# Rescheduling a Gram product and a triangular solve among the matmuls of a fused delta-rule attention and two-layer MoE kernel

## The chip, the cores and the metric

The kernel runs on one core of one Trainium2 chip. The metric is the time of one execution on the device in microseconds; the figure before is the median of three executions.

## The reference

A delta-rule attention (4 batches, 8 heads, 768 tokens, head dimension 48) feeds two dense layers that act on each token:

```python
for t in range(S):
    kt, vt, bt = (k_n[:, :, t], v[:, :, t], beta[:, :, t, None])
    y[:, :, t] = np.einsum('bhd,bhde->bhe', q[:, :, t], state)
    v_old = np.einsum('bhde,bhd->bhe', state, kt)
    state = state + bt[:, :, :, None] * np.einsum('bhd,bhe->bhde', kt, vt - v_old)
...
h = np.maximum(x @ w_in, 0.0)              # 384 -> 2048
x = (h * h @ w_out)                        # 2048 -> 384
...
h = np.maximum(np.maximum(x @ w1, x @ w2), x @ w3)   # 384 -> 768
out = h @ w_out                            # 768 -> 384
```

## The kernel before

The 768 tokens are cut into 12 chunks of 64 (numbered 0 to 11). Inside a chunk the recurrence becomes a triangular system: the Gram matrix K K^T of the chunk, scaled by beta and by the key norms, is inverted, and the inverse is used in a handful of small matmuls. All dense matmuls run as three products of high and low parts, which is why tiles come in pairs (`xh`, `xl`; `gh`, `gl`).

The main loop runs over the chunks c. In round c, `moe_a(c)` runs the first dense layer on chunk c, while the attention of chunk c+1 and the preparation of later chunks are threaded between its steps. `moe_a` has eight blocks of the hidden dimension. `s1(f)` (L599) is 18 matmuls into one of two banks `p1`; ACT takes them through relu, square and a rounding to `gh` (L605 to L607) and DVE forms `gl` (L608), after which the bank is free. `s2(f)` (L619) multiplies `gh` and `gl` into the accumulator `px`, two blocks later. At the end DVE transposes `px` to `xs` (L639), which frees `px` and is stored.

`moe_a` yields after every `s1` and `s2`; the yields are numbered: step 1 follows s1(0), 2 s1(1), 3 s1(2), 4 s2(0), 5 s1(3), 6 s2(1), 7 s1(4), 8 s2(2), 9 s1(5), 10 s2(3), 11 s1(6), 12 s2(4), 13 s1(7), 14 s2(5), 15 s2(6), and step 16 follows s2(7) and the transposes to `xs`. `steps` takes lists of step numbers, each with a generator, and advances the generator once for each occurrence of the step. `pin` then orders the instructions of PE and DVE exactly as they were written; ACT, POOL and the DMA queue of SP are ordered by the scheduler.

The generators that matter here:

- `attention(c+1)`: loads of the inverse (`load_x`, POOL's queue, L348 and L366), products with the state (st0), `zz` (a DVE transpose `xT`, L419, and the matmuls `pZ`, L426, copied to `z` by ACT, L427), `ww` (the matmuls `pW`, L436, which read `xT` and `z`), `mm_u` (L491), st2 (L543, L521; DVE then adds to `Sb`, L528, and copies `yy`, L553), st3 (PE transposes `yy` to `pT`, L561; the results are `xh` and `xl`, L564 and L565). In even rounds these stand at steps 1, 2, 4, 6, 8, 11, 13; in odd rounds at 1, 2, 5, 7, 10, 12, 14 (round 9: 6 and 8 in place of 5 and 7).
- `kkps`: four Gram products (two chunks, two halves), each in two pieces. The first piece is 64 small matmuls into two banks `pk` and `pq` (L182), an ACT copy (L198) and a DVE multiplication with the mask (L199); the second is the stores on SP's queue (L186, L206). The banks come from the pool `ps_at` of two, which the attention uses as well.
- `solve32(g)`: the inverse of the 32x32 diagonal blocks of two chunks. Its first piece loads the Gram blocks to `M32` (L312, SP's queue). The second is the preparation `prep`: the diagonal `ss` (L247), a square root on ACT (L218), a selection on POOL (L236), some short DVE operations and two of 1024 elements (L247 to L255). Then come 30 pairs of DVE operations (L292, L293), a memset and a last scaling (L295, L296), with a PE transpose of the norms (`pt`, L279) among them; then the result goes to DRAM (`xt`, L329), from where the next round's `load_x` fetches it.

Rounds 3, 5 and 7 run `kkps` and the first piece of `solve32`; rounds 4, 6 and 8 run the rest of that solve; rounds 5, 7 and 9 fetch its result. Round 2 has a list of its own. After chunk 11 the second layer (L1023, L1040) runs on the tokens alone.

Of the kernel before, what the change touches and what calls it, by code (L numbers as in the profile page):

```python
# [35 lines left out]
HALVED = [(c, c + 1) for c in range(0, NC, 2)]  # L36
# [3 lines left out]
def delta_moe(ctx, tc, kc, ab, kt, vt, beta, beta32, beta16, kq, w_in, w_out, w1, w2, w3, w_out2, out):  # L40
# [124 lines left out]
    def kkp_load(c, p, dma=nc.sync):  # L165
        k = kcts[nk[0] % len(kcts)]
        nk[0] += 1
        kcs[c, p] = k
        i = dma.dma_start(k, two(kc, c, p).rearrange("p b q t s -> p (b q) t s"))
        for j in kc_after:  # L170
            behind(i.ins, j)

    def kk_matmul(c, p, ps_, swap=1):

        k = kcs.pop((c, p))
        pk, pq = (ps_[0].tile([128, U2, C], F32, name=n, tag=ps_[1]) for n in ("pk", "pq"))
        for u in range(U2):
            for i, ps in enumerate((pk, pq)):
                for t in range(2):
                    r = slice(64 * t, 64 * t + D)  # L180
                    o = 64 * (t ^ i * swap)
                    pe.matmul(ps[o:o + 64, u], k[r, u, 0], k[r, u, i], start=True, stop=True)  # L182
        return pk, pq

    def kk_store(c, p, kk, dma=nc.sync):
        dma.dma_start(kk_d[c // 2].rearrange("t j c u i -> (t j) c u i")[:, c % 2, U2 * p:U2 * p + U2], kk)  # L186

    def kkps(cs, ps_, dma=nc.sync):

        todo = [(c, p) for c in cs for p in range(2)]  # L190
        ahead = len(kcts) - (len(kcts) < 4)
        for n in range(min(ahead, len(todo))):
            kkp_load(*todo[n], dma)
        for n, (c, p) in enumerate(todo):
            ks = kss[nk[1] % len(kss)]
            nk[1] += 1
            pk, pq = kk_matmul(c, p, ps_[n % len(ps_)])
            kk_ends[0] = act.copy(ks[:, 0], pk).ins  # L198
            kk_ends[1] = vec.tensor_mul(out=ks[:, 1], in0=pq, in1=mask.unsqueeze(1).broadcast_to([128, U2, C])).ins  # L199
            for i in mul_after:  # L200
                behind(kk_ends[1], i)
            yield
            kk_store(c, p, ks[:, 0], dma)

            for t in range(2):
                dma.dma_start(p_d[c][64 * t:64 * t + 64, U2 * p:U2 * p + U2], ks[64 - 64 * t:128 - 64 * t, 1])  # L206
            if n + ahead < len(todo):
                kkp_load(*todo[n + ahead], dma)
            yield
# [63 lines left out]
    def behind(ins, before):  # L273

        tc.add_manual_dep(ins, before.name, mybir.DependencyInfo(mybir.DependencyClass.NoSync, mybir.DependencyReason.DATA), reason="order")
# [378 lines left out]
    def steps(main, *others):  # L654

        due = [0.0] * len(others)
        for n, _ in enumerate(chain((None,), main)):
            pin()
            for i, (rate, g, *_) in enumerate(others):
                due[i] += rate.count(n) if isinstance(rate, list) else rate * (n > 0)  # L660
                while due[i] >= 1.0:
                    due[i] -= 1.0
                    next(g, None)
                    pin()
        for rate, g, *keep in others:
            for _ in () if keep else g:
                pin()
# [7 lines left out]
    def w3load(ws):  # L675
        todo = []

        def turned():
            if after:
                after[:], abs_after[:] = last_gl, last_gh  # L680
            raw, i, fs = todo.pop(0)
            turn(raw, wh[i][:, :, fs], wl[i][:, :, fs], vec)

        for i in ws:
            w = (late if i < 2 else wb).tile([128, 2, KD, F2], F32R, name=f"w3_{i}", tag="ABC"[i])
            wh[i], wl[i] = w[:, 0], w[:, 1]
            for f in range(NF2):
                fs = slice(128 * f, 128 * (f + 1))
                todo.append((fetch(w3s[i][:, :, 256 * f:256 * (f + 1)], (KD, 128), nc.sync), i, fs))
                if len(todo) > 1:  # L690
                    turned()
                yield
        turned()
# [29 lines left out]
    def part(g, n):  # L723
        for _ in range(n):
            next(g, None)
            yield
# [5 lines left out]
    if True:  # L732
# [20 lines left out]
        def solve32(g, load=(nc.sync, nc.sync), landing=0):  # L753
            M, a, ready, norm = start32(g, load) if g else begun
            for _ in range(landing):
                yield
            if landing:
                prep_after[:] = last_gl
            nm = ready()
            if not g:  # L760
                normed.append(lambda: norms_at.append(norm(nm)))
            yield
            for n, i in enumerate(solve(vec, M, 32, 64 * len(HALVED[g]), a, tmp32, g < 2)):
                for j in solve_after:
                    behind(i.ins, j)
                ops.append(i.ins)
                if g and n == (24 if g == 1 else 8):
                    norm(nm)
                yield
            i = finish32(g, M)  # L770
            if i:
                ops.append(i)

        def later(n, g):
            for _ in range(n):
                yield
            yield from g
# [3 lines left out]
        def weights(first, each):  # L781
            n = first
            while queue:
                if last_gl[0] and last_gl[0] not in gls:
                    gls.append(last_gl[0])
                after[:] = gls[-2:-1] or last_vec[:1]
                words(n)
                n = each
                after.clear()
                prep_after[:] = solve_after[:] = parted[-1:]  # L790
                yield

        at, p1 = (ps_at, "at"), (ps_s1, "p1")
# [168 lines left out]
        KK = {1: 2, 3: 3, 5: 4, 7: 5}  # L962
        ahead_ = {}
        for c in range(NC):
            extra = []
            if c == 0:
                solve_next = solve32(1, (pool, pool))
                extra += [(11 / 15.0, later(3, attention(1))), (list(range(17)), weights(2, 2)), (4.0, later(20, part(solve_next, 10)))]
            elif c == 1:
                pinned.update({first_matmul.ins.engine: None, last_gl[0].engine: None})  # L970
                first_solve = [0] * 3 + [1 + n * 18 // 20 for n in range(20)]
                extra += [(first_solve, solve_next), ([13, 19, 22, 25, 27, 28, 30], attention(2))]
                ahead_[2] = solve32(2, landing=1)
                extra += [([9, 10, 16, 17, 20, 21, 24, 25], kkps(HALVED[2], (at,))), ([28], ahead_[2], True)]
                solve_after[:] = last_vec
                kc_after[:] = raws[-1:]
                prep_after.clear()
            elif c + 1 < NC:
                extra.append(([1, 2, 5 + c // 9, 7 + c // 9, 10, 12, 14] if c % 2 else [1, 2, 4, 6, 8, 11, 13], attention(c + 1)))
            if c == 2:  # L980
                kc_after.clear()
                solve_after.clear()
            if c in ahead_:
                extra.append(([2] + [3 + n * 12 // 32 for n in range(32)] if c == 2 else [3 + n * 12 // 33 for n in range(33)], ahead_[c]))
            if c > 1 and c in KK:
                extra.append(([4, 5, 6, 7, 9, 10, 11, 12], kkps(HALVED[KK[c]], (at,))))
                ahead_[c + 1] = solve32(KK[c], landing=1)
                extra.append(([12], ahead_[c + 1], True))
            if c == 9:
                after[:] = last_gl  # L990
                load_w3s = w3load((0, 1))
            if 9 <= c < NC - 1:
                extra.append((0.4, part(load_w3s, 6)) if c > 9 else (0.8, later(6, part(load_w3s, 6))))
            if c == NC - 1:
                pr.close()
                wb = ctx.enter_context(tc.tile_pool(name="wb", bufs=1, side="right", reuse_waits="tile"))
                first = []
                extra.append((0.6, chain(load_w3s, w3load((2,)))))
                extra.append((0.5, later(2, x2_steps(0, wb, first))))
            steps(moe_a(c, gp, c == 1), *extra)  # L1000
# [114 lines left out]
```

## Time and profile before

| | |
|---|---|
| three executions | 911.59, 913.41, 913.48 us; median 913.41 |
| the profiled execution | 915.94 us, its span 913.8 |
| PE busy / DVE busy | 871.0 / 478.5 us |
| ACT busy / POOL busy | 387.8 / 135.7 us |

The span is the time between the first and the last instruction that the profile shows; a few microseconds lie around it. Rounds 3 to 9 take about 47 us each: round 3 starts near 208 us in the span, round 4 near 259, round 5 near 303, round 9 near 488. "Busy" counts compute instructions alone. A row that ends in `[1.32 <-DVE ...]` says that the engine idled 1.32 us before it and what it waited for.

### The profile page before, as it was taken

The page shows a single profiled execution, that of the slowest core. Times are in us where ns is not written, and L with a number is a line of the kernel's source. Part 1 is how long each engine was busy: PE and PEld are TensorE (multiplying, and loading weights), DVE is VectorE, ACT ScalarE, POOL GpSimd, SP SyncE. Part 2 cuts the span into 40 slices and gives each one's busy share as a digit, 9 for nine tenths or more (in the row PEclk, how much of TensorE's full clock was granted, in tenths as well). Part 3 has the DMA queues.
Part 4 walks back from the last instruction along what each step waited for, and adds up shares of the span by engine and source line. Part 5 has one row for each costly group of instructions (what it writes and reads, how often), then busy time and mean ns, then how long its engine had stood idle before and what let it go on. Part 6 is the DMA issues. An engine that isn't in the chain of part 4 may idle for free.

```text
span 913.8 us, 26365 instructions
## 1 busy us (share of the span) xinstructions
PE 871.0 (95%) x11414; PEld 845.0 (92%) x11414; DVE 478.5 (52%) x1069; ACT 387.8 (42%) x825; POOL 135.7 (15%) x226
## 2 busy tenths in 40 slices
PE   4589899999999999999999999999999999999998
PEld 4588899999998999999999899999999999999997
DVE  5887985694349524962496354566232332323221
ACT  6568745453445343534453566554121221222211
POOL 5041201223312231223122400001000000000000
PEclk8759999999999999999999999999999999999999
DMA  9968446525652566245715441434010101000000
GB/s 264 360 169 255 116 100 168 125 65 144 179 117 66 136 174 129 64 112 158 147 58 123 116 124 37 122 105 137 29 36 27 35 27 35 10 27 9 18 18 35
DMA packets 114035, 95.36 MB, mean 104 GB/s; under 512 B 69880, under 2 KB 95240, under 8 KB 113920
## 3 DMA queue, kind: packets, MB, share of 16 engines
q1 hardware_dynamic: 95232, 55.41, 23.0%
q0 software_dynamic: 11584, 32.64, 13.3%
q10 hardware_dynamic: 7104, 5.64, 2.0%
q8 instruction: 89, 1.46, 0.7%
q14 instruction: 26, 0.21, 0.1%
HBM read 70.45 MB, written 22.77 MB: 102 GB/s over the span
## 4 chain that ended last, share of the span: by engine, by line
PE 74%; DVE 14%; DMA 4%; ACT 3%; issue 3%; POOL 1%; ACTq 0%; DVEq 0%; POOLq 0%
PE p L1023 25%; PE p L599 16%; PE px L619 16%; PE po L1040 8%; DVE buf L292 3%; DVE buf L293 3%; DVE gl L608 2%; PE pk L182 2%; PE pU L491 1%; PE pY L543 1%; PE pA L467 1%; DMA raw<-in_moe_w_out_dram 1%; DMA p<-ksr 1%; PE pW L436 1%; DMA xb<-xt 1%
## 5 line engine op out<-in xcount | busy, mean ns | idle before, releaser
L1023 PE MATMUL p<-x_h,w 128*128 128x384 f32 x864 | 220.2, 336 | 0.0
L619 PE MATMUL px<-wout,gh 128*128 128x384 f32 x768 | 200.4, 342 | 1.5 <-ACT gh L607 0.8
L599 PE MATMUL p<-xh,win_h 128*128 128x256 f32 x576 | 169.3, 294 | 3.1 <-DVE gl L608 2.6
L599 PE MATMUL p<-xl,win_h 128*128 128x256 f32 x576 | 163.9, 284 | 0.2 <-DVE xl L565 0.2
L599 PE MATMUL p<-xh,win_l 128*128 128x256 f32 x576 | 163.8, 284 | 0.0
L1023 PEld LDWEIGHTS p<-x_h,w 128*128 128x128 f32 x864 | 156.2, 188 | 0.0
L1023 PE MATMUL p<-x_l,w 128*128 128x384 f32 x432 | 145.2, 336 | 0.0
L608 DVE TENSOR_TENSOR gl<-p,gh 128x512 fp32r<-128x512 f32 x96 | 66.2, 689 | 145.1 <-ACT gh L607 141.4
L619 PEld LDWEIGHTS px<-wout,gh 128*128 128x128 f32 x768 | 135.4, 190 | 3.4 <-issue 1.2
L619 PE MATMUL px<-wout,gl 128*128 128x384 f32 x384 | 129.4, 337 | 0.0
L605 ACT ACTIVATE p<-p 128x512 f32<-128x512 f32 x96 | 55.9, 582 | 172.1 <-PE p L599 169.4
L599 PEld LDWEIGHTS p<-xh,win_h 128*128 128x128 f32 x576 | 110.8, 192 | 6.7 <-DVE gl L608 3.3
L599 PEld LDWEIGHTS p<-xl,win_h 128*128 128x128 f32 x576 | 111.0, 193 | 0.5 <-DVE xl L565 0.4
L599 PEld LDWEIGHTS p<-xh,win_l 128*128 128x128 f32 x576 | 111.0, 193 | 0.0
L1029 DVE TENSOR_TENSOR mx<-p,mx 128x384 f32<-128x384 f32 x48 | 26.7, 557 | 128.1 <-PE p L1023 128.0
L1023 PEld LDWEIGHTS p<-x_l,w 128*128 128x128 f32 x432 | 81.2, 188 | 0.0
L1031 ACT CAST hh<-mx 128x384 fp32r<-128x384 f32 x48 | 24.6, 513 | 125.6 <-DVE mx L1030 125.6
L619 PEld LDWEIGHTS px<-wout,gl 128*128 128x128 f32 x384 | 72.7, 189 | 0.1
L293 DVE TENSOR_TENSOR buf<-buf 128x30 f32<-128x30 f32 (+9 forms) x180 | 59.7, 332 | 6.1
L292 DVE TENSOR_TENSOR buf<-buf 128x30 f32<-128x30 f32 (+9 forms) x180 | 59.4, 330 | 5.1
L607 ACT CAST gh<-p 128x512 fp32r<-128x512 f32 x96 | 56.4, 587 | 2.6
L606 ACT ACTIVATE p<-p 128x512 f32<-128x512 f32 x96 | 56.0, 583 | 2.7
(169 smaller groups left out, 1305.7 us busy)
## 6 DMA issues: line engine op xcount, KB each, us to landing
kq<-in_kc_dram POOLq DMA_DIRECT2D x20, 448.0 KB, 5.2
raw<-in_moe_w_dram SPq DMA_DIRECT2D x18, 384.0 KB, 3.7
raw<-in_moe_w_out_dram SPq DMA_DIRECT2D x16, 384.0 KB, 4.2
p<-p POOLq DMA_DIRECT2D x22, 256.0 KB, 4.0
rawp<-in_moe_w_in_dram SPq DMA_DIRECT2D x12, 384.0 KB, 7.0
v<-in_vt_dram POOLq DMA_DIRECT2D x24, 192.0 KB, 2.9
ktp<-in_kt_dram POOLq DMA_DIRECT2D x24, 192.0 KB, 4.0
x<-xs SPq DMA_DIRECT2D x48, 96.0 KB, 3.0
```

The source lines that it names most:

```text
L292: eng.tensor_tensor(out=tv, in0=col.unsqueeze(2).broadcast_to([u, k, l]), in1=row.unsqueeze(1).broadcast_to([u, k, l]), op=ALU.mult)
L293: i = eng.tensor_tensor(out=of_, in0=of_, in1=tv, op=ALU.add)
L599: pe.matmul(p1[:, j], w[:, k, f], x[c][:, k], start=n == 0 and j == 0, stop=n == 8, skip_group_check=True)
L605: act.activation(out=p1, in_=p1, func=AF.Relu)
L606: act.activation(out=p1, in_=p1, func=AF.Square)
L607: last_gh[0] = act.copy(gh, p1).ins
L608: last_gl[0] = vec.tensor_sub(out=gl, in0=p1, in1=gh.bitcast(F32)).ins
L619: g = pe.matmul(px[:, h, 0:DM], x[:, j, hs], w, start=f == 0 and i == 0, stop=f == NF - 1 and i == 2, skip_group_check=True)
L1023: pe.matmul(p, w[i][:, k, fs], x[:, k], start=n == 0, stop=n == 8)
L1029: vec.tensor_max(out=t, in0=ps[1], in1=t)
L1031: act.copy(hh[:, f], t2)
L1040: pe.matmul(po[:, 0:DM], x[:, f, js], w[:, f], start=i == 0, stop=i == 17)
```

## The change

Rounds 3, 5 and 7 (`c > 1 and c in KK`) and rounds 4, 6 and 8 (`c in ahead_`, other than 2) get new lists of steps:

```diff
-                extra.append(([2] + [3 + n * 12 // 32 for n in range(32)] if c == 2 else [3 + n * 12 // 33 for n in range(33)], ahead_[c]))
+                extra.append(([2] + [3 + n * 12 // 32 for n in range(32)] if c == 2 else [1 + n * 14 // 32 for n in range(32)], ahead_[c]))
             if c > 1 and c in KK:
-                extra.append(([4, 5, 6, 7, 9, 10, 11, 12], kkps(HALVED[KK[c]], (at,))))
+                extra.append(([4, 5, 6, 7, 8, 9, 9, 10], kkps(HALVED[KK[c]], (at,))))
                 ahead_[c + 1] = solve32(KK[c], landing=1)
-                extra.append(([12], ahead_[c + 1], True))
+                extra.append(([11, 15], ahead_[c + 1], True))
```

The matmuls of the third and fourth Gram product go from steps 9 and 11 to 8 and 9; their stores from 10 and 12 to 9 and 10; the load of `M32` from 12 to 11. The preparation, which was the first item of the next round (step 3), stands at step 15 of rounds 3, 5 and 7. The solve's operations in the next round are spread over steps 1 to 14 in place of 3 to 14. No instruction is added or removed.

DVE from the end of round 3, before (`xl` is the last operation of the attention, `xs` the transposes of `px`, `v` the products of st0):

```order
L565 TENSOR_TENSOR xl<-pT,xh 128x3x128 x2
L639 STREAM_TRANSPOSE xs<-px 128x384 x2
L608 TENSOR_TENSOR gl<-p_3991,gh 128x512
L608 TENSOR_TENSOR gl<-p_4030,gh 128x512
L458 TENSOR_TENSOR v<-v,normT 128x384
L471 TENSOR_TENSOR v<-v,pA 128x384
L458 TENSOR_TENSOR v<-v,normT 128x384
L471 TENSOR_TENSOR v<-v,pA 128x384
L608 TENSOR_TENSOR gl<-p_4131,gh 128x512
L247 COPY ss<-buf 128x32
```

and with the change:

```order
L565 TENSOR_TENSOR xl<-pT,xh 128x3x128 x2
L247 COPY ss<-buf 128x32
L219 SCALAR_TENSOR_TENSOR s_3977<-s_3977 128x32
L220 RECIPROCAL r<-s_3977 128x32
L221 TENSOR_TENSOR r<-r,ss 128x32
L222 SCALAR_TENSOR_TENSOR nm<-r,s_3977 128x32
L228 TENSOR_TENSOR s_3977<-nm 128x32
L229 RECIPROCAL a_3803<-s_3977 128x32
L230 SCALAR_TENSOR_TENSOR r<-b_3804,a_3803 128x32
L237 TENSOR_TENSOR buf<-buf,r 128x1024
L255 TENSOR_SCALAR a_3803<-r 128x32
L639 STREAM_TRANSPOSE xs<-px 128x384 x2
```

The preparation has moved from behind the third `gl` of round 4 to a place ahead of round 3's `xs`.

DVE around `xT` of round 4, before:

```order
L237 TENSOR_TENSOR buf<-buf,r 128x1024
L255 TENSOR_SCALAR a_3907<-r 128x32
L292 TENSOR_TENSOR buf<-buf 128x30
L293 TENSOR_TENSOR buf<-buf 128x30
L292 TENSOR_TENSOR buf<-buf 128x58
L293 TENSOR_TENSOR buf<-buf 128x2x29
L419 STREAM_TRANSPOSE xT<-x_4025 128x256
```

and with the change:

```order
L608 TENSOR_TENSOR gl<-p_4157,gh 128x512
L292 TENSOR_TENSOR buf<-buf 128x150
L293 TENSOR_TENSOR buf<-buf 128x6x25
L292 TENSOR_TENSOR buf<-buf 128x168
L293 TENSOR_TENSOR buf<-buf 128x7x24
L419 STREAM_TRANSPOSE xT<-x_4041 128x256
```

Between the third `gl` and `xT` there stood the whole preparation and two pairs of the solve; now two later pairs stand there.

ACT around the Gram copies of round 3 (`buf<-pk` and `big<-pk`, the third and fourth product), before:

```order
L445 COPY xb<-pW 32x8x32 x4
L607 CAST gh<-p_3540 128x512
L605 ACTIVATE p_3618<-p_3618 128x512
L606 ACTIVATE p_3618<-p_3618 128x512
L607 CAST gh<-p_3618 128x512
L198 COPY buf<-pk 128x512
```

and with the change:

```order
L445 COPY xb<-pW 32x8x32 x4
L607 CAST gh<-p_3540 128x512
L198 COPY buf<-pk 128x512
L605 ACTIVATE p_3654<-p_3654 128x512
L606 ACTIVATE p_3654<-p_3654 128x512
L607 CAST gh<-p_3654 128x512
L198 COPY big<-pk 128x512
```

The third copy has moved ahead of the copies of s1(5), and the fourth stands right behind them, ahead of the copies of `pU`.

## Rows read from the trace of the kernel before

**Rows 1.** The page, busy time of each engine (share of the span), instructions.

```profile
PE 871.0 (95%) x11414; PEld 845.0 (92%) x11414; DVE 478.5 (52%) x1069; ACT 387.8 (42%) x825; POOL 135.7 (15%) x226
```

**Rows 2.** Waits of PE, whole span: us in total, times, longest.

```profile
PE pW L436 <- DVE buf L292: 3.9, 3, 1.3
...
PE pT L561 <- DVE yy L553: 1.7, 3, 0.7
PE pZ L426 <- DMA xb<-xt: 1.3, 2, 0.8
```

**Rows 3.** Timeline of DVE in round 4: start, us, operation.

```profile
270.12 0.18 DVE L247 COPY ss<-buf 128x32 f32<-128x32 f32 x1
...
274.59 0.18 DVE L255 TENSOR_SCALAR a<-r 128x32 f32<-128x32 f32 x1
...
275.55 0.44 DVE L419 STREAM_TRANSPOSE xT<-x 128x256 f32<-128x256 f32 x1
```

**Rows 4.** Timeline of PE: a stall of round 3, two waits of round 4.

```profile
224.61 0.25 PE L426 MATMUL pZ<-xb,k 32*32 32x32 f32 x3 [1.20 <-issue]
...
276.13 0.74 PE L436 MATMUL pW<-k,xT 32*32 32x32 f32 x64 [1.32 <-DVE buf L292]
...
296.70 0.49 PE L561 MATMUL pT<-ident,yy 128*128 128x128 f32 x3 [0.72 <-DVE yy L553]
```

**Rows 5.** Groups of DVE, 274 to 306 us: busy, mean ns | idle before.

```profile
L293 DVE TENSOR_TENSOR buf<-buf 128x30 f32<-128x30 f32 (+14 forms) x30 | 10.0, 332 | 1.0
...
L608 DVE TENSOR_TENSOR gl<-p,gh 128x512 fp32r<-128x512 f32 x5 | 3.4, 683 | 0.0
```

**Rows 6.** Timeline of DVE from round 3 into round 4.

```profile
255.01 1.02 DVE L565 TENSOR_TENSOR xl<-pT,xh 128x384 fp32r<-128x384 f32 x2 [0.39 <-ACT xh L564]
258.99 1.05 DVE L639 STREAM_TRANSPOSE xs<-px 128x384 f32<-128x384 f32 x2 [2.96 <-PE px L619]
262.99 0.69 DVE L608 TENSOR_TENSOR gl<-p,gh 128x512 fp32r<-128x512 f32 x1 [2.95 <-ACT gh L607]
265.14 0.69 DVE L608 TENSOR_TENSOR gl<-p,gh 128x512 fp32r<-128x512 f32 x1 [1.46 <-ACT gh L607]
```

**Rows 7.** Timeline of PE in round 4: first matmuls of s1(2) and of s2(0).

```profile
265.20 0.39 PE L599 MATMUL p<-xh,win_h 128*128 128x256 f32 x1
...
267.46 0.52 PE L619 MATMUL px<-wout,gh 128*128 128x384 f32 x2
```

**Rows 8.** Round 3: PE's fourth Gram product, then SP's queue.

```profile
244.21 0.27 PE L182 MATMUL pk<-big 48*64 48x64 f32 x2
...
246.65 0.51 SPq L186 DMA_DIRECT2D kk<-big  x1
...
250.70 5.55 SPq L312 DMA_DIRECT2D buf<-kk  x4
```

**Rows 9.** DMA, 236 to 262 us: busy tenths (0.65 us each); all loads of L312.

```profile
DMA  0000196999788995698997578999984996000008
...
DMA to landing us min/median/max: 3.4/6.1/8.7
```

**Rows 10.** Timeline of ACT in round 3: the copies of `pW`.

```profile
233.28 1.49 ACT L445 COPY xb<-pW 32x256 f32<-32x256 f32 x4
```

**Rows 11.** Rounds 8 to 9: DVE, SP's queue, PE, and landing times.

```profile
488.68 1.23 DVE L296 TENSOR_TENSOR buf<-buf,a 128x1024 f32<-128x1024 f32 x1
...
494.57 5.06 SPq L94 DMA_DIRECT2D raw<-in_moe_w_dram  x3
...
504.85 0.74 PE L426 MATMUL pZ<-xb,k 32*32 32x32 f32 x62 [0.56 <-DMA xb<-xt]
...
xb<-xt POOLq DMA_DIRECT2D x4, 64.0 KB, 7.9
```

**Rows 12.** Windows: PE, PEld, DVE, ACT, POOL busy; PE's clock; DMA share; GB/s.

```profile
224.60:227.00 2.40, 2.39 (x10) 2.35 (x11) 1.04 (x2) 0.86 (x2) 0.00 (x0) 0.57 0.25 90
274.80:276.20 1.40, 0.08 (x8) 0.10 (x11) 1.26 (x7) 0.00 (x0) 0.00 (x0) 1.00 0.00 0
```

## The prediction, made before the changed kernel was run

> **What bounds the kernel now.** I read the page first: PE is busy 871.0 of 913.8 us [rows 1], so only what keeps PE idle can move the time. The list of PE's waits comes next. Most of its longest entries belong to the start-up and to rounds 0 to 3, which the change doesn't reach. In rounds 4 to 9 three of any size remain [rows 2]: pW behind DVE, three times, 3.9 us; pT behind DVE's yy, three times, 1.7 us; pZ behind a DMA, two pieces of one stall, 1.3 us. The reader should see that all three stand on one chain, the solve: together 6.9 us, 0.75% of the time.
>
> The first is named after L292, but pW reads no solve result. Round 4's timelines show what it waits for: DVE runs the preparation from 270.12 to 274.77, two pairs of the solve, and only then xT, at 275.55 [rows 3]; pW starts at 276.13, right after it, 1.32 us late [rows 4]. The second is the same backlog 20 us later: from 274 to 306 us all 60 operations of the solve lie on DVE (30 of L293 cost 10.0 us, those of L292 as much), and no gl finds DVE waiting for it (idle 0.0 us) [rows 5]; yy comes late and pT waits 0.72 us [rows 4]. Rounds 6 and 8 repeat both. The third is the result of round 8's solve: the last scaling ends at 489.91, the result goes to DRAM and comes back, and pZ of round 9 starts in full only at 504.85 [rows 11].
>
> **The preparation, moved to step 15.** It is the same ten DVE operations, 4.65 us from 270.12 to 274.77 [rows 3], with one ACT and one POOL operation inside that span. Its new place is behind xl, which ends at 256.03, and ahead of xs [rows 6]. There DVE was idle: 2.96 us before xs and 2.95 before the first gl of round 4 [rows 6]. Worked through for round 3: preparation 256.03 to 260.7, xs (1.05 us) to 261.75, and gl is ready for DVE at 262.99, as before. So xs is 1.7 us later and gl not at all. Who waits for xs is px: s2(0) starts at 267.46 [rows 7], 5.7 us later. So the move costs nothing if M32 is there at 256.0. Cover beyond that: gl must have read its bank before s1(2) starts at 265.20 [rows 7]; with 4.65 + 1.05 + 0.6 us ahead of that, the preparation may start as late as 258.9. From there each microsecond costs PE one, in three rounds, and ACT's square root and POOL's selection hold those queues too.
>
> **Is M32 there?** The fourth Gram product stands at 244.21, its store at 246.65, the loads at 250.70, all four issued by 256.25 [rows 8]; the DMA engines fall quiet after slice 34, at 258.1 [rows 9]. So the loads take 7.4 us from the first issue. Now the product starts after s2(2), the third product and s1(5), that is one s1 and one s2 and a little waiting earlier, near 238.5: 5.7 us before. Loads then start at 245.0 and end at 252.4, 3.6 us before DVE is free. Bounds: the last is issued by 250.2, and the slowest landing of any such load is 8.7 us [rows 9], which gives 258.9, just the limit; the quickest, 3.4, gives 253.6. I take 252.4 to 254, since the transfers around it are the same ones. Cost 0.
>
> The Trainium skill, "DMA: Bandwidth & Descriptors", section "Queues, rings and completion order", speaks against this: each DMA engine takes turns, packet by packet, between the queues that have work, so SP's loads would share the engines with POOL's of the same steps. If that doubled the 7.4 us, the loads would end at 259.8, 0.9 us past the limit, and three rounds would lose 2.7 us: a gain of 4.1 in place of 6.8. The rows show the engines nearly full already around these loads, so the 7.4 us hold such sharing in part.
>
> **The Gram products, moved.** PE's work is the same 64 matmuls, in another place: 0. The third now follows s2(2), at 235.1, and takes the bank that pW held; ACT's copies of pW end at 234.77 [rows 10], 0.3 us earlier. A late copy would cost PE at most about that, three times under 1 us. The fourth follows one s1 later, and ACT and DVE clear its banks before mm_u. SP's stores move with them; nothing on that queue waits longer, as it idled. The keys of each are loaded behind the product two before it, well ahead. Cost 0, upper bound 1 us.
>
> **The solve, spread from step 1.** Three pairs now stand ahead of the second gl of round 4. Two pairs took from 274.71 to 275.55, 0.84 us [rows 3], so three take some 1.4: after the first gl (to 263.6) DVE is free at 265.0, and the second gl's input arrives for 265.14 [rows 6]. No loss. After the third gl two pairs at a mean of 0.66 us (19.9 us over 30, [rows 5]) and xT's 0.44 put xT at 271.9; pW may start at 274.8. It has 2.9 us to spare, so **the pW wait goes: 3.9 us**.
>
> At yy, DVE is relieved of the preparation (4.65) and of five early pairs (at least 0.84 for the first two, some 2.5 in all) and has two more pairs ahead of it (1.5): it comes over 5 us earlier, or when its inputs arrive. It was late by 0.72 at most. **The pT wait goes: 1.7 us.**
>
> The last scaling of round 8 ends earlier by the same 5 us, of which PE's own advance in that round takes 1.7 (1.3 + 0.4): some 3.3 us earlier as PE sees it, against a stall of 1.3 us. On SP's queue, though, one of the weight loads that stood ahead of the xt stores now stands behind the x stores, with the three that are there [rows 11], while pZ's loads are in flight (7.9 us from issue to landing [rows 11]). Three issue over 5.06 us, so one more is worth up to 1.7 us of the same engines. 3.3 - 1.7 = 1.6 is still more than 1.3; between 0 and 1.3 I take **1.2 us**.
>
> The clock adds nothing: it stayed at 1.00, the 2.4 GHz level, through the pW wait [rows 12]. In round 3, which keeps its stall, PE ran at 0.57 for 2.4 us after one of 1.2 us [rows 4, 12]; a new stall of that kind would cost about 1.2 + 1.0 us.
>
> **Sum.** 3.9 + 1.7 + 1.2 = 6.8 us. After round 9 PE has no gap worth naming, so nothing gives the time back. The profiled execution took 915.94 us (span 913.8, 2.1 around it): 909.1. It stands 2.5 above the median of 913.41; against that I predict **906.6 us**.
>
> **Rivals.**
>
> (a) *The loads collide, by the rule above*: 4.1 us gained, 909.3. For it: DMA slices of 9 all through 246 to 256 us [rows 9]. Against: 7.4 us is measured among such traffic. Chance 0.10.
>
> (b) *A DMA takes the wait's place*. The DVE waits go (5.6), but pZ of round 9 waits longer as the extra weight load pushes its rows back by the 1.7 us: 5.6 - 1.7 = 3.9, 909.5. One stall of the kind of round 3's (2.2 us) elsewhere gives about the same, 908.8. For it: landing times of 7.9 us [rows 11]. Against: the stores it needs are issued first. Chance 0.16.
>
> (c) *The change doesn't do what it says*: pW waits for something other than xT, such as z or its loads, and finds the next wait at once, and the gain at pT and pZ is eaten by the copies' 1 us and a stall: within 1.8 us of 913.4. Against: xT and pW touch in the rows. Chance 0.08.
>
> (d) *Slower*: the preparation, now at the head of DVE's queue, waits for M32 and holds xs and gl, and PE stands at s1(2). It decides from the landing: past 258.9 each microsecond costs three, past 261.2 the 6.8 are spent, past 261.8 the kernel is slower by 0.2%. If M32 lands at 262, it is 3.1 x 3 = 9.3 - 6.8: 915.9. For it: the order puts ten DVE operations in front of everything in round 4, and one load can hold them. Against: no load of this line took over 8.7 us. With a DVE or ACT wait that I don't see, chance 0.11.
>
> **How the numbers follow.** The forecast has 0.55; (a) and (b) add 0.26. A measurement of this kernel can tell about 0.2%, 1.8 us, from no change. Faster by more: 0.81; within: 0.08; slower: 0.11. The range begins at 904.6, where the pZ wait goes whole and the median falls 1.9 us low by the scatter of the three runs, and ends at 911.5, which takes in (a) and (b) with 2 us to spare; outside are (c) and (d), 0.19.
>
> **What would show it.** Right: in the changed profile L247 starts at once behind xl, without idle for a DMA, and ends before gl's input; no pW and no pT wait on DVE in rounds 4, 6 and 8; idle before gl reappears there; pZ of round 9 starts within 0.3 us. The span falls by 6 to 7 us and PE's busy time doesn't change. Wrong: a wait of ss on kk's load, p (L599) behind gl in rounds 4, 6 or 8, pq behind ACT's xb in rounds 3, 5 or 7, a clock under 1.00 after a new stall, or a pZ wait in round 5, 7 or 9 of over 1.5 us.

## The result and the profile after

The changed kernel takes 905.2 us (median of five, 903.85 to 905.88) where the kernel before took 913.41 (911.59 to 915.19): a ratio of 0.9912, interval 0.9893 to 0.993. That is 8.2 us faster; 6.8 were forecast. The profiled execution took 903.85 us with a span of 902.1, against 915.94 and 913.8.

The page's first part, to be read against [rows 1]:

```profile
PE 868.1 (96%) x11414; PEld 843.6 (94%) x11414; DVE 479.4 (53%) x1069; ACT 387.7 (43%) x825; POOL 135.8 (15%) x226
```

The same work lies in a shorter span. PE's waits from 205 to 560 us, rounds 3 to 9 and a little more, first of the kernel before (us in total, times, longest), then of the changed one:

```profile
PE pW L436 <- DVE buf L292: 3.9, 3, 1.3
PE pT L561 <- DVE yy L553: 1.7, 3, 0.7
PE pZ L426 <- DMA xb<-xt: 1.3, 2, 0.8
PE pZ L426 <- issue: 1.2, 1, 1.2
PE px L619 <- issue: 0.7, 1, 0.7
```

```profile
core 0 of [0], span 902.1 us
engine line waited for: us in total, times, longest us
```

There is no row under the second heading: the view lists no wait of PE in these rounds any more. The three waits of [rows 2] are gone, and so are the two by issue, of which more below.

The timeline of DVE from round 3 into round 4 of the changed kernel answers to [rows 6] and [rows 3]:

```profile
252.76 1.02 DVE L565 TENSOR_TENSOR xl<-pT,xh 128x384 fp32r<-128x384 f32 x2 [0.39 <-ACT xh L564]
255.18 0.19 DVE L247 COPY ss<-buf 128x32 f32<-128x32 f32 x1 [1.40 <-issue]
...
259.66 0.18 DVE L255 TENSOR_SCALAR a<-r 128x32 f32<-128x32 f32 x1
259.75 1.04 DVE L639 STREAM_TRANSPOSE xs<-px 128x384 f32<-128x384 f32 x2
260.73 0.69 DVE L608 TENSOR_TENSOR gl<-p,gh 128x512 fp32r<-128x512 f32 x1
```

The preparation fills what was idle, and the first gl follows xs at once. One thing is not as forecast: the preparation starts 1.4 us behind xl. The row puts that down to issue, but it was the load of M32, as shown below. Later in the round (xT of DVE; then pW and pT of PE; then the groups of DVE from 272 to 304 us):

```profile
269.17 0.44 DVE L419 STREAM_TRANSPOSE xT<-x 128x256 f32<-128x256 f32 x1
```

```profile
272.52 0.75 PE L436 MATMUL pW<-k,xT 32*32 32x32 f32 x64
...
291.86 0.82 PE L561 MATMUL pT<-ident,yy 128*128 128x128 f32 x6
```

```profile
L608 DVE TENSOR_TENSOR gl<-p,gh 128x512 fp32r<-128x512 f32 x6 | 4.1, 690 | 5.7 <-ACT gh L607 5.7
```

xT ends 2.9 us ahead of pW. The six transposes to pT run in one piece, where a wait cut them into three and three before [rows 4]. In that stretch DVE now idles 5.7 us ahead of gl, where it idled 0.0 [rows 5]: the backlog is gone.

The lengths of the rounds put a place to the gain. A round is counted here from its first product with the state (the first row of L467 in PE's timeline) to the next round's, in us:

| round | 3 | 4 | 5 | 6 | 7 | 8 | 9 |
|---|---|---|---|---|---|---|---|
| before, first profile | 50.40 | 44.50 | 48.48 | 44.37 | 47.53 | 44.47 | 43.81 |
| before, second profile (e0) | 47.46 | 44.50 | 48.78 | 44.34 | 48.09 | 44.47 | 43.12 |
| changed | 47.42 | 42.21 | 47.41 | 42.21 | 47.42 | 42.28 | 42.20 |

Rounds 4, 6 and 8 lose 2.1 to 2.3 us in both comparisons, 6.6 together. Round 9 loses 1.6 or 0.9. Rounds 3, 5 and 7 differ between the two executions of the same kernel by up to 2.9, but round 5 is long in both (48.48 and 48.78 against 47.41). The even rounds are some 3 us shorter than the odd ones, so the "about 47 us" named ahead of the prediction holds for the odd ones only.

### The profile page after: what moved, and what is told of

The parts are those of the page before. It is cut to its first block, busy times and chain, and to the rows that moved or that the text cites. A ratio compares the mean times of both kernels' runs of the same rounds, so it can differ in the third digit from the quotient of the medians.

```text
span 902.1 us, 26366 instructions
## 1 busy us (share of the span) xinstructions
PE 868.1 (96%) x11414; PEld 843.6 (94%) x11414; DVE 479.4 (53%) x1069; ACT 387.7 (43%) x825; POOL 135.8 (15%) x226
## 3 DMA queue, kind: packets, MB, share of 16 engines
q8 instruction: 89, 1.46, 0.7%
## 4 chain that ended last, share of the span: by engine, by line
PE 86%; DVE 6%; ACT 3%; DMA 3%; issue 2%; POOL 0%; DVEq 0%; ACTq 0%; POOLq 0%
PE p L1023 25%; PE p L599 21%; PE px L619 20%; PE po L1040 8%; PE pY L543 2%; PE pU L491 2%; PE pk L182 1%; PE pA L467 1%; DMA p<-ksr 1%; PE pW L436 1%; PE pZ L426 1%; DVE gl L608 1%; PE pT L561 1%; DMA ktp<-in_kt_dram 1%; PE pq L182 1%
```

## The experiments

Theory A: the preparation, 4.65 us of DVE ahead of xT, is the backlog that PE waits for; moving it into DVE's idle time at the end of the round before is the whole gain, and it lasts as long as M32 is there in time. The rivals: that the spread of the solve, the earlier Gram products or a chance stall make the gain. Each experiment ran beside the kernel before on the same chip (medians 913.68, 914.56 and 913.94 us in the three sets).

**e0, the kernel before again.** No edit.

> The kernel before, once more, to see which of its waits come back. Theory A (the gain is the solve's backlog on DVE): the waits of pW (1.3 us) and pT (0.4 to 0.7) in rounds 4, 6, 8 and of pZ in round 9 (1.3) stand there again, and the stall of round 3 (pZ, 1.2 us by issue, then a clock of 0.57), which the change cannot reach, may be absent: then round 3 takes 47.4 us, not 50.4, and the span is near 911. Rival B (that stall belongs to the order before and the change removed it): round 3 takes 50.4 us again.

913.74 us, ratio 1.0008 (0.9991 to 1.0025). The waits of pW and pT stand there to a tenth of a microsecond; the stall of round 3 does not. PE's waits from 215 to 540 us:

```profile
PE pW L436 <- DVE buf L292: 3.9, 3, 1.3
PE pT L561 <- DVE yy L553: 1.6, 3, 0.7
PE px L619 <- issue: 1.4, 2, 1.0
PE pZ L426 <- DVE gl L608: 0.5, 1, 0.5
```

So round 3's stall isn't the change's to remove: it comes in some executions. The stall of px in round 5 is another matter. It stands in both profiles of the kernel before (0.7 and 1.0 us), and with the runs that follow it turns out to go with the order of the solve. And the pZ stall of round 9 was 0.5 us here, not 1.3.

**e1, without the spread.** The Gram products and the preparation are moved; the solve stays at steps 3 to 14.

```diff
-[1 + n * 14 // 32 for n in range(32)]
+[3 + n * 12 // 32 for n in range(32)]
```

> The change with the solve's operations left at steps 3 to 14, so that only the Gram products and the preparation are moved. Theory A (the 4.65 us of preparation ahead of xT are the backlog): no wait of pW or pT on DVE is left, rounds 4, 6, 8 take 42.2 to 42.5 us, and the time is within 1 us of the changed kernel's 905.2. Rival B (the spread over 14 steps is what frees DVE): pT waits remain (0.5 to 0.9 us each) and pZ of round 9 too, and the time is 907.5 to 909.

905.75 us, 0.9904 (0.9887 to 0.992), within 1 us of the change. Rounds 4, 6, 8 and 9 take 42.27, 42.21, 42.34 and 42.20 us. For these four rounds the spread does nothing that shows: A. Round 5 takes 48.14 us, though, against 47.41 in the changed kernel, with 0.3 us of idle at px; what the spread does there is taken up below.

**e2, the spread alone.** From the kernel before:

```diff
-[3 + n * 12 // 33 for n in range(33)]
+[1 + n * 14 // 33 for n in range(33)]
```

> The kernel before with the solve, preparation first, spread over steps 1 to 14 of the next round; Gram products as before. Theory A: DVE's 2.9 us of idle ahead of the third gl are filled, but the preparation and five pairs still stand ahead of xT, so pW waits about as before (1.0 to 1.8 us, three times), pT's wait goes (0.9 each) and pZ's in part: 909 to 911. Rival B (the spread is what matters): the waits go and the time is 905 to 907.

911.99 us, 0.9977 (0.9964 to 0.999): a gain of 1.7 us, and A's side in the time, though 1 us above its range. That pW would wait as before was wrong: the wait is elsewhere. DVE in round 4, then PE:

```profile
261.00 0.18 DVE L247 COPY ss<-buf 128x32 f32<-128x32 f32 x1
...
265.48 0.18 DVE L255 TENSOR_SCALAR a<-r 128x32 f32<-128x32 f32 x1
...
266.44 0.69 DVE L608 TENSOR_TENSOR gl<-p,gh 128x512 fp32r<-128x512 f32 x1
...
268.83 0.56 DVE L471 TENSOR_TENSOR v<-v,pA 128x384 f32<-128x384 f32 x1
```

```profile
268.31 0.83 PE L426 MATMUL pZ<-xb,k 32*32 32x32 f32 x64 [1.19 <-DVE v L471]
269.44 0.28 PE L279 MATMUL pt<-ident,nm 128*32 128x128 f32 x1 [0.30 <-DVE v L471]
```

With the preparation two steps earlier in the same round, gl and the four operations of st0 stand behind it, and these clear the two banks that pZ and pt need. The waits at pW and pT are gone, and 1.5 us at pZ and pt have come in their place. Round 4 still takes 45.43 us, longer than before, since PE's clock fell after that wait (0.76, then 0.64, in the windows below). So each of the two places tried in round 4, step 3 and step 1, costs PE a wait. Rounds 4, 6 and 8 take 45.43, 43.98 and 45.40 us, 1.5 more together than in e0; what this kernel gains stands in rounds 5, 7 and 9 (47.42, 47.42 and 42.21).

**e3, the Gram products back.** From the changed kernel:

```diff
-[4, 5, 6, 7, 8, 9, 9, 10], kkps
+[4, 5, 6, 7, 9, 10, 11, 12], kkps
-([11, 15], ahead_[c + 1], True)
+([12, 15], ahead_[c + 1], True)
```

> The change with the Gram products back at steps 4 to 12, so that the load of M32 starts some 5.7 us later while the preparation stays at step 15. Theory A as predicted (the four loads take 7.4 us from the first issue): M32 is there at 258.1 in round 3, 0.8 us ahead of the limit, and the time is within 1 us of 905.2. Rival B (the loads take 11 to 12.5 us, as the changed kernel's trace suggests): ss waits until 262 or 263, PE stands at s1(2) for want of a bank for 3 to 4 us in rounds 4 and 6, perhaps 8, and the time is 911 to 917, the gain gone.

906.24 us, 0.9908 (0.9889 to 0.9928). SP's queue, DVE and PE around round 4:

```profile
249.64 5.74 SPq L312 DMA_DIRECT2D buf<-kk  x4
```

```profile
254.02 1.02 DVE L565 TENSOR_TENSOR xl<-pT,xh 128x384 fp32r<-128x384 f32 x2 [0.39 <-ACT xh L564]
258.36 0.19 DVE L247 COPY ss<-buf 128x32 f32<-128x32 f32 x1 [3.32 <-DMA buf<-kk]
...
263.90 0.65 DVE L608 TENSOR_TENSOR gl<-p,gh 128x512 fp32r<-128x512 f32 x1
```

The loads took 8.7 us (249.64 to 258.36), between the two expectations and nearer the first. The preparation waits 3.32, 3.00 and 3.22 us in rounds 3, 5 and 7, and PE waits 0.33 us in round 4, no listed time in round 6 and 0.23 in round 8 at s1(2). The forecast's cover behind xl is 258.9 - 256.03 = 2.87 us; past it 3.32 leaves 0.45: the limit is where it was put, within about 0.1. So the Gram products' move saves some tenths of a microsecond in two of the three rounds.

**e4, the Gram products alone.** From the changed kernel, with the preparation back in the next round:

```diff
-[1 + n * 14 // 32 for n in range(32)]
+[3 + n * 12 // 33 for n in range(33)]
-([11, 15], ahead_[c + 1], True)
+([11], ahead_[c + 1], True)
```

> Only the Gram products and the load of M32 are moved, as in the change; the preparation stays at step 3 of the next round and the solve at steps 3 to 14. Theory A (the place of the preparation is what counts): pW's and pT's waits stand as before, and the time is within 1.5 us of 913.5. Rival B (an earlier M32 alone frees something): 910 or less.

914.02 us, 1.0003 (0.9985 to 1.002); rounds 4, 6 and 8 take 44.32, 44.32 and 44.74 us. No gain.

**e5, rounds 3 to 6 alone.** Each of the three lists takes its old form where `c == 7` or `c == 8`:

```diff
+([3 + n * 12 // 33 for n in range(33)] if c == 8 else [1 + n * 14 // 32 for n in range(32)])
+([4, 5, 6, 7, 9, 10, 11, 12] if c == 7 else [4, 5, 6, 7, 8, 9, 9, 10])
+[12] if c == 7 else [11, 15]
```

> The change in rounds 3 to 6 alone; rounds 7 and 8 as before. Theory A (each even round gives 2.2 us of its own, and round 9 about 1.2 through the earlier result of round 8): round 8 takes 44.4 us and round 9 43.1 to 43.8 again, rounds 4 and 6 42.2, and the time is 905.2 + 3.4, 908 to 909.2. Rival B (the gain sits in one place, or the time is given back later): 905 to 906.5 or above 911.

907.28 us, 0.9928 (0.9902 to 0.9953). Rounds 4 and 6 take 42.23 and 42.21 us, round 8 44.33, round 9 42.64. Each even round brings its own: round 8 in its old form takes 2.1 us more than in the changed kernel. Round 9's part was 0.4 here, so the time stayed 0.7 us under the expectation.

**e6, step 15 alone.** From the kernel before, the smallest edit that moves the preparation:

```diff
-[3 + n * 12 // 33 for n in range(33)]
+[3 + n * 12 // 32 for n in range(32)]
-([12], ahead_[c + 1], True)
+([12, 15], ahead_[c + 1], True)
```

> The kernel before with one thing changed: the preparation at step 15. The Gram products, the load and the solve's steps 3 to 14 stay. Theory A (the preparation's place carries the whole gain, and the rest of the change is worth 1 us at most): ss waits some 3 us for the load, PE loses 0 to 0.4 us a round at s1(2), no pW or pT wait on DVE, 905.5 to 907.5. Rival B (two of the three parts are needed together): a pT wait or a longer s1(2) wait comes back, 908 to 911.

906.07 us, 0.9916 (0.989 to 0.9942). The preparation waits 2.19, 2.31 and 3.38 us for its load in rounds 3, 5 and 7, and the one wait of PE that is listed for rounds 3 to 8 is this:

```profile
PE p L599 <- DVE gl L608: 0.4, 1, 0.4
```

It stands in round 8, where 3.38 is past the cover. This one part carries the gain to within 1 to 2 us (905.2 and, in e9, 904.33 for the whole change), which the intervals don't separate. Round 5 takes 47.88 us here, 0.5 more than in the changed kernel.

**e7, the load later still.** From the changed kernel:

```diff
-[4, 5, 6, 7, 8, 9, 9, 10], kkps
+[4, 5, 6, 7, 9, 10, 12, 13], kkps
-([11, 15], ahead_[c + 1], True)
+([14, 15], ahead_[c + 1], True)
```

> The change with the fourth Gram product at step 12, behind st2 (the third at 9), so the load of M32 starts some 4 us later still than with the old places, and the preparation waits for it at the head of DVE's queue at step 15. Theory A (past a limit of 2.9 us behind xl each microsecond costs PE one, in rounds 4, 6 and 8): ss starts 6 to 7.5 us behind xl, PE stands 3 to 4.5 us at s1(2) in each of the three rounds behind gl, and the time is 914 to 919, slower than before. Rival B (PE has other work or the load comes sooner since the DMA engines are less full): under 910.

917.48 us, 1.0034 (1.0011 to 1.0056): slower than before. DVE, PE's wait in round 4 and its waits from 205 to 560 us, and windows of the same stretch as the first rows (busy PE, PEld, DVE, ACT, POOL; PE's clock; DMA share; GB/s):

```profile
253.50 1.02 DVE L565 TENSOR_TENSOR xl<-pT,xh 128x384 fp32r<-128x384 f32 x2 [0.39 <-ACT xh L564]
260.09 0.19 DVE L247 COPY ss<-buf 128x32 f32<-128x32 f32 x1 [5.56 <-DMA buf<-kk]
```

```profile
266.33 0.39 PE L599 MATMUL p<-xh,win_h 128*128 128x256 f32 x1 [2.57 <-DVE gl L608]
```

```profile
PE p L599 <- DVE gl L608: 6.9, 3, 2.6
PE pq L182 <- DVE Sb L528: 1.7, 3, 0.6
```

```profile
263.70:266.30 2.60, 0.06 (x5) 0.00 (x0) 2.60 (x6) 0.28 (x1) 0.57 (x2) 1.00 0.69 188
266.30:267.00 0.70, 0.67 (x4) 0.68 (x5) 0.60 (x4) 0.00 (x0) 0.00 (x0) 0.80 1.01 287
267.00:269.00 2.00, 2.00 (x12) 2.00 (x11) 1.83 (x6) 0.00 (x0) 0.00 (x0) 0.50 1.17 239
269.00:271.00 2.00, 2.00 (x12) 2.00 (x12) 1.86 (x5) 0.70 (x2) 0.00 (x0) 0.72 0.61 89
```

The preparation waits 5.56 us; less the cover of 2.87 that is 2.69, and PE waits 2.57. But round 4 takes 46.37 us, 4.16 more than in the changed kernel: after the wait PE ran at 0.50, the 1.2 GHz level, for two microseconds and at 0.72 for two more. The rival on the slower side is real, and it costs more than its wait. Not all of this run's time is the load's, however: behind st2 the moved product waits 0.6 us for a bank, in each of rounds 3, 5 and 7, and these take 0.9 to 1.1 us more than in the changed kernel, 2.8 together. Without them the time would be near 914.7 (an estimate, 917.48 - 2.8), level with the kernel before.

**e8 and e9, the first Gram product behind pZ, and the change again.** e8's edit to the changed kernel:

```diff
-[4, 5, 6, 7, 8, 9, 9, 10], kkps
+[5, 6, 6, 7, 8, 9, 9, 10], kkps
```

> The change with the first Gram product one step later, behind pZ (steps 5, 6, 6, 7, 8, 9, 9, 10), so that its stores and the next load of keys no longer run while pZ of rounds 3, 5 and 7 starts. Theory A (the stalls of about 1 us by issue, seen at pZ of round 3 and px of round 5 in some executions only, come from those transfers): they are absent, rounds 3, 5 and 7 take 47.4 us in the profile, and the time is 903.5 to 905, 0.5 to 1.5 us under the changed kernel's. Rival B (they come from something else, or the second product two half-steps later brings a wait for a bank of its own): the same or slower, 905 to 907.

> The changed kernel again, on the chip and in the rounds of the one above, for the comparison. All theories: 904.5 to 906.5 beside 913.5 for the kernel before; rounds 4, 6, 8 and 9 take 42.2 us, and rounds 3 and 5 take 47.4 or, with a stall by issue, up to 49 us.

e9: 904.33 us, 0.9894 (0.988 to 0.9908), rounds as in the table. e8: 906.22 us, 0.9919 (0.9903 to 0.9935). PE's waits of e8 from 205 to 560 us:

```profile
PE pq L182 <- ACT k L427: 1.9, 3, 0.6
```

No stall by issue was seen in this execution, but there was none in e9 either. Behind pZ the product wants the bank that pZ has just filled, and waits 0.63 us in each of three rounds for ACT to empty it; rounds 3, 5 and 7 take 48.2 us. Rival B, and a worse order than the change's. None of these kernels beats the changed one.

## Why the prediction was right

**What bounded the kernel.** Right. PE was the bound, the three waits were the gain, and the label of the first was misleading in the way described: pW waited for xT. Once xT ended ahead of it, pW started behind s2(1) without idling.

**The preparation at step 15.** Right, and it is the term that counts: with it alone the kernel takes 906.07 us (e6), without it 914.02 (e4) or 911.99 (e2), where the kernel before takes 913.7 to 914.6 beside them. Its place cost PE nothing: gl of round 4 came before it was needed.

**Is M32 there?** Right in the outcome, wrong in the size: here the forecast's reading failed. The forecast took 7.4 us from the first issue to the end of the loads, read from where the DMA engines fall quiet (258.1). The landings in that same trace say more: the last load of round 3, issued at 255.57, landed at 259.0, 8.3 us after the first issue and 0.1 past the limit that the forecast had put at 258.9. At the old place the loads took 7.2 to 8.7 us until the preparation started in rounds 3 and 5 of e3 and e6, and some 10 in round 7. In the changed kernel they took longer still. In round 5 the wait names the load; the loads were issued from 332.43 us:

```profile
343.63 0.19 DVE L247 COPY ss<-buf 128x32 f32<-128x32 f32 x1 [0.22 <-DMA buf<-kk]
```

That is 11.2 us. In round 3 the landings of the four loads show it, though the row of L247 says issue:

```profile
L312 SPq DMA_DIRECT2D buf<-kk x4: 321/1774/2429, 242.6 to 247.1; - x4
DMA to landing us min/median/max: 6.0/7.4/8.0
```

The last was issued at 247.09 and landed 8.0 us later, at 255.10; the preparation started at 255.18, 12.5 us after the first issue and 1.4 behind xl. Counted from xl, that is 257.4 in the forecast's round 3, where 252.4 to 254 had been taken. In e9 no preparation waited. Starting the loads 5.5 us sooner in round 5 than in e3 (29.28 us into the round against 34.74) brought M32 forward by only 2.8 (40.48 against 43.26): 11.2 us of loading, with the DMA engines at a mean share of 1.09, against 8.5 with 0.79.

The direction is that of the Trainium skill's rule ("DMA: Bandwidth & Descriptors", "Queues, rings and completion order"), by which each DMA engine takes turns between the queues that have work. The trace agrees in so far as the loads slowed where the engines were fuller; which transfers slowed them, no run shows. A doubling to 14.8 us was not seen. The cover absorbed the delay: 1.4 of 2.87 us. So it was the cover and not the 7.4 us that made "cost 0" come true.

**The Gram products.** Right: PE saw no bank wait. They are worth little: e6 and e3 take 0.9916 and 0.9908 of the time of the kernel before, the change 0.9912 and 0.9894, so between nothing and 2 us, with intervals that overlap. Their use is cover for the load.

**The spread.** The forecast used its order for the arguments at xT and yy; e1 shows that pW and pT lose their waits without it. But it is not without effect. Round 5 takes 47.41 to 47.45 us in the changed kernel, e2, e3, e5 and e9, all with the solve of round 4 spread from step 1 (e7 and e8, spread as well, have bank waits of their own there and no px stall), and 47.88 to 48.78 in all five profiles with the solve at steps 3 to 14 (before, e0, e4, e1, e6). The difference is the px stall of round 5, up to 1.0 us of idle. The list of waits in the trace before showed it (0.7 us), and the forecast, which named three waits "of any size" in rounds 4 to 9, left it out. That the spread removes it rests on these twelve profiles, one execution each; in the times of e1 and the changed kernel (905.75, 905.2) it does not stand clear of the noise.

**The sum.** 6.8 us forecast, 8.2 measured, and 9.6 in e9 (904.33 against 913.94). Two terms were too small and one was missing. pW's wait is 1.3 us in the list, but from the first matmul of s2(1) to pW it takes 3.57 us before and 2.18 after: 1.39. From pT to the next s2 it is 1.46 and 0.57: 0.89, where the list says 0.72 for round 4. So a wait cost a little more than the idle time listed for it; what the rest is made of isn't shown. Over the three rounds these stretches give 6.4 of the 6.6 us that the rounds lost, in place of 5.6. The third term, 1.2 us for round 9, came out at 0.4 to 1.6 in the four profiles that still have the old round 8 (before, e0, e4, e5). The missing one is round 5: 1.1 and 1.4 us in the two profiles of the kernel before. With round 7 (0.1 and 0.7) the rounds account for the 9.6 us between the spans of e0 and the changed kernel (911.7, 902.1): 6.6 + 0.9 + 1.4 + 0.7. The 11.7 us from the first profile's span, where the forecast named 6 to 7, must not be read as the gain: 3.0 of them are round 3's stall with its slow clock. PE's busy time fell by 2.9 us in these two profiles (871.0 to 868.1), where no change was named.

**The rivals.** (a) fired in part, without cost; with it came one of the listed signs of being wrong, a wait of ss on kk's load. (b) and (c) did not occur. (d) is real and was put at the right point: e3 and e7 found the limit within 0.2 us. Its price was too low, as the clock was left out: round 4 of e7 lost 4.16 us for a wait of 2.57. The same goes for a stall of round 3's kind, priced at 2.2 us: round 3 is 2.9 us longer with it (50.40 against 47.46).

## What to carry to other kernels

When a matmul waits for an engine in order, look at what is queued ahead of the instruction it reads, and move the longest piece that is ready early into the engine's idle time a round before; here that carried most of the gain, and spreading the rest at most some 1 us more. Before such a move write down how long the piece may wait for its own input, by the landing of the last transfer: here the cover was 2.87 us, the load used up to half of it, and 2.7 us past it the whole gain was gone. Sum the gain from stage lengths of two profiles of the same kernel, not from one span.

## What was not expected of the hardware

- The clock after a short wait is not a function of its length alone. pW's wait of 1.3 us left it at 1.00 [rows 12], round 3's of 1.2 us by issue was followed by 0.57 in one execution, and in e1 the same stall (1.22 us) by 1.00. e7's three waits at s1(2), 1.75 to 2.57 us, were all followed by a stretch at 0.50. After e2's wait of 1.19 us it fell as well; windows of e2, columns as above:

```profile
267.00:268.40 1.40, 0.21 (x3) 0.09 (x3) 1.30 (x4) 0.00 (x0) 0.00 (x0) 1.00 0.44 97
268.40:271.00 2.60, 2.30 (x73) 2.19 (x74) 2.39 (x8) 1.13 (x5) 0.00 (x0) 0.76 0.02 6
271.00:274.00 3.00, 3.00 (x17) 3.00 (x17) 2.77 (x10) 0.58 (x1) 0.00 (x0) 0.64 0.00 0
```

- The stall by issue in round 3 came at the same instruction each time, behind 61 of pZ's 64 matmuls, in four executions (before, e1, e3, e5) and not in the others with that order, while the DMA engines were full (a share of 0.93 to 1.01; it was 0.95 to 1.02 in executions without the stall too). e1's row:

```profile
225.40 0.25 PE L426 MATMUL pZ<-xb,k 32*32 32x32 f32 x3 [1.22 <-issue]
```

What the DMA records show beside it is a transfer of the kind "instruction": a packet of 16 KB on queue q8, 89 or 90 of them in an execution. DMA queues by kind (packets, MB, share of 16 engines), in e1 from 222 to 223 us, then in e0, which has no such stall, from 221 to 222:

```profile
q8 instruction: 1, 0.02, 8.4%
```

```profile
q8 instruction: 1, 0.02, 8.2%
```

In the four executions with the stall this packet started 8.8 to 9.3 us into round 3, in the eight others 6.9 to 7.6, and PE went on 1.3 to 1.5 us after the packet's end. The px stall of round 5 looks the same: the packet starts 9.0 to 9.8 us into the round in the five executions that have it and 7.3 to 7.8 in the seven that don't, and PE goes on 1.3 to 1.6 us after its end. So PE probably stands there for want of its own next instructions. No run moved that packet by itself, so this is not shown, and neither is why the packet comes late; in round 5 it does so with the solve at steps 3 to 14. The one attempt to move other transfers away (e8) brought a wait of its own and couldn't tell.
